# A transformer block in float32: fixed probability buffers taken in turn, with the order of two writes declared

## The chip, the core and the metric

The kernel runs on one core of a Trainium2 chip, as one launch. The core has a matrix engine (TensorE, "PE" in the profile; its weight loads are listed apart as "PEld"), a vector engine (VectorE, "DVE"), an activation engine (ScalarE, "ACT"), a general one (GpSimd, "POOL") and a sync engine ("SP"), which here issues all transfers to and from memory. Each engine works through its own list of instructions in order; one engine waits for another by semaphores. The metric is the time of one execution in device microseconds.

## The reference

One block with adaptive layer norm, for 2048 tokens of width 512: multi-head attention with 32 heads of width 16, then a two-layer network with the Mish activation and an inner width of 1792. All in float32.

```python
mod = (_silu(c) @ w_mod).reshape(c.shape[0], 6, 1, -1)
sa, ca, ga, sb, cb, gb = (mod[:, 0], mod[:, 1], mod[:, 2], mod[:, 3], mod[:, 4], mod[:, 5])
h = _layernorm(x, axis=-1) * (1 + ca) + sa
x = x + ga * _A_ref(h, A_wqkv, A_wo)      # softmax attention
h = _layernorm(x, axis=-1) * (1 + cb) + sb
x = x + gb * _B_ref(h, B_w1, B_b1, B_w2)  # Dense, Mish, Dense
```

What the change touches lies in the attention: scores = q k / 4, p = softmax(scores), o = p v.

## The kernel before, in words

**Precision.** Most operands are split into a high and a low part (names ending in `h` and `l`, or in `_h` and `_l`), and a product is made of three matmuls of such parts (`mm3`, L111). GpSimd, ScalarE and VectorE make the parts (`hi_copy` L89, `lo_sub` L97).

**Stages.** A set-up (L309 to L446) normalizes x, makes the first slices of k, q and v and stores them in DRAM scratch (`kscr`, `qscr`, `vscr`). At its end `constants()` (L405) issues transfers that fill rows of `qa` (L398), `qscr` (L409) and `vscr` (L410) with zeros, all copied from one tile `zer`. The tiles of the set-up lie in a pool `lp` that is closed at its end. Then the pools `kq2` (three more `ka` tiles) and `ap` (L451) are opened, in the space that `lp` left. The pool `ap` is opened with `reuse_waits="tile"`: an instruction that first writes a tile of it waits for what last used the memory there, whether of `ap` or of `lp`.

The main loop (L1212) goes over steps t = -20 to 513. Steps 0 to 511 are 32 iterations n of 16 steps: an iteration is four heads and 512 query tokens, a step on average one block of 128 key tokens. A step has

- four scores, so that two steps make the eight of four heads and two key blocks (`score`, L503): a matmul of k and q into one bank of `ring` and ScalarE's exponential (L510) from it into a probability buffer `pr`;
- four maxima (`max_tile`, L462) for the iteration that comes 20 steps later: a matmul (L470) into a bank of `ring` and VectorE's maximum over it (L472) into the tile `mx`, from which the rows of maxima are later made that the scores subtract;
- the values' product of step t - 2 (`pv`, L517): four matmuls (L525) that read the four `pr` buffers and the values `vg`;
- a part of other work: projections, weight preparation and the two-layer network of an earlier block of 512 tokens, cut into units (`queue`, `next_part`).

Steps -20 to -1 have maxima and whole units alone (`whole_units`), among them the values' projections (`v_unit`, L262; matmuls by L126).

**Order.** The order is written out by hand (`tc.manual_schedule()`, L49): each engine runs its instructions in the order in which the program lists them, and the hooks `at(h, ...)` set at which half step something is issued. So nothing is moved by a planner; what can differ is what an instruction waits for, and where the pool puts a tile.

**Banks.** `ring` (L144) has six banks of 128 x 512 float32, taken in turn by scores, maxima and a few others. A product that takes a bank waits until what last read it has done so.

**The probability buffers.** There are four heads in an iteration. For head 2j + s there are 3 + s buffers (14 in all), taken in turn by the pool: each call of `ap.tile(..., tag=..., bufs=3 + s)` gives the next. A new exponential into a buffer waits for the values' product that last read it and for the exponential that last wrote it. After the loop, `tail()` (L876) takes eight more tiles of the same tags for the last block's y and xn.

Of the kernel before, what the change touches and what calls it, by code (L numbers as in the profile page):

```python
# [8 lines left out]
F32 = mybir.dt.float32  # L9
# [9 lines left out]
def adaln_block(ctx: ExitStack, tc: tile.TileContext, x, wqkv, wo, w1, b1, w2, c, w_mod, out):  # L19
    nc = tc.nc  # L20
    P = 128
    S, D = x.shape[1], x.shape[2]
# [5 lines left out]
    TB = 512  # L28
# [4 lines left out]
    T = 16 * NIT  # L33
# [66 lines left out]
    def layernorm(pool, xt, xn, eng="v"):  # L100
        st = pool.tile([P, 6], F32, tag="ln_st", name="ln_st", bufs=4)
        mv = pool.tile([P, 2], F32, tag="ln_mv", name="ln_mv", bufs=4)
        rs = pool.tile([P, 2], F32, tag="ln_rs", name="ln_rs", bufs=4)
        nc.vector.bn_stats(out=st, in_=xt)
        nc.vector.bn_aggr(out=mv, in_=st)
        nc.gpsimd.tensor_scalar(rs[:, 0:1], mv[:, 1:2], 1.0, EPS, op0=ALU.mult, op1=ALU.add)
        nc.gpsimd.tensor_tensor(rs[:, 1:2], rs[:, 0:1], nhalf, op=ALU.pow)
        eng = nc.vector if eng == "v" else nc.gpsimd
        return lambda: eng.tensor_scalar(xn, xt, mv[:, 0:1], rs[:, 1:2], op0=ALU.subtract, op1=ALU.mult)
# [28 lines left out]
    def pe_run():  # L138
        while pe_queue:
            mm_go(pe_queue.pop(0))  # L140
# [6 lines left out]
    def ring(w=1):  # L147
        if w == 2 and ring_at[0] % 2:
            ring_at[0] += 1
        b = ring_at[0] % NRING  # L150
        ring_at[0] += w
        return ring_t[:, b, :] if w == 1 else ring_t[:, b:b + 2, :]

    def bank(tag="ms"):
        return ring() if tag == "ring" else ps.tile([P, TB], F32, tag=tag, name="bk", bufs=1)
# [153 lines left out]
    with ExitStack() as es:  # L309
# [28 lines left out]
        e = lp.tile([P, DK], F32, name="sil_e")  # L338
# [39 lines left out]
        pr, pm = [], ring()[:, :2 * DK].rearrange("p (i k) -> p i k", k=DK)  # L378
# [72 lines left out]
    ap = ctx.enter_context(tc.tile_pool(name="ap", bufs=1, reuse_waits="tile"))  # L451
# [46 lines left out]
                        mt[o:o + 8, :].bitcast(F32))  # L498
        at(2 * (16 * n + 16 - PRO) + 3, put)

    pts = {}

    def score(n, j, s, kc):  # L503
        def product():
            kt, qt = ka[(2 * n + j) % NR], qa[(2 * n + j) % NR]
            p_ = ring()
            nc.tensor.matmul(p_, kt[64 * s:64 * s + 64, kc * P:(kc + 1) * P], qt[64 * s:64 * s + 64, :],  # L507
                             start=True, stop=True)
            pr = ap.tile([P, TB], F32, tag=f"p{2 * j + s}", name="pr", bufs=3 + s)
            e = nc.scalar.activation(pr, p_, AF.Exp, scale=SCALE)  # L510
            pts[16 * n + kc, 2 * j + s] = pr
            return e
        return product
# [67 lines left out]
    def evac_last(ps_):  # L581

        ot, od, rb = mst["last"]
        oh, ol = o_hl[NB - 1]
        r = slice(64, P)
        dn, on = ps_
        pick = mst["pick"]
        nc.tensor.matmul(dn[r, :], pick[:, 1, :], ot, start=True, stop=True)
        nc.tensor.matmul(on[r, :], pick[:, 0, :], ot, start=True, stop=True)
        nc.vector.reciprocal(rb[r], dn[r, :])  # L590
        nc.vector.tensor_mul(od[r], on[r, :], rb[r])
        hi_copy("v", oh[r, DK - 1, :], od[r])
        lo_sub("v", ol[r, DK - 1, :], od[r], oh[r, DK - 1, :])
# [67 lines left out]
    def load_w2(f):  # L661
        return load_split("w2", NA, w2scr[f])
# [14 lines left out]
    def put_h(hh, hl, acc, k, tail):  # L677
        hf = mst["p"].tile([P, TB], F32, tag="ee", name="hf2", bufs=2)
        nc.scalar.activation(hf, acc, AF.Identity, scale=modc[:, 3, k:k + 1], bias=modc[:, 2, k:k + 1])
        hi_copy("p", hh[:, k, :], hf)  # L680
        lo_sub("v" if tail else "p", hl[:, k, :], hf, hh[:, k, :])

    def up_mms(acc, w, hh, hl):
        mm3(acc, [w1v(w, 0, k) for k in range(DK)], [w1v(w, 1, k) for k in range(DK)],
            [hh[:, k, :] for k in range(DK)], [hl[:, k, :] for k in range(DK)], "b")

    def mish(f, acc, tail):

        mp = mst["p"]
# [176 lines left out]
    def w1_tail(f):  # L866
        i, j = divmod(f % 8, 2)
        return load_w1(f) if i == 1 else half_tile(ka[(1, 0, 2, 3)[i]], j, w1scr[f])
# [7 lines left out]
    def tail():  # L876

        oh, ol = o_hl[last]
        mp = mst["p"]
        y, xn = [], []  # L880
        for v in (y, xn):
            for i in range(4):
                v.append(ap.tile([P, D], F32, tag=f"p{i}", name="y", bufs=3 + i % 2))
        for i in range(4):
            r = 4 * last + i
            nc.sync.dma_start(y[i], x[r * P:(r + 1) * P, :])
        for f in range(4, 8):
            w1s[f] = w1_tail(f)
        accs4 = [bank("ms"), bank("acc")] + [None, None]

        def wo_mms(i, ks):
            s = slice(i * P, (i + 1) * P)
            seq = [(l, r, k) for l, r in ((oh, 0), (oh, 1), (ol, 0)) for k in ks]
            for j, (l, r, k) in enumerate(seq):
                nc.tensor.matmul(accs4[i], l[:, k, s], wos[k][:, r, :], start=(k == 0 and j == 0),
                                 stop=(k == 3 and j == 2))

        wo_mms(0, (0, 1, 2))
        t = ring(2)
        evac_last([t[:, i, :] for i in range(2)])  # L900
        wo_mms(1, (0, 1, 2))
        for i in (2, 3):
            accs4[i] = bank("ring")
            wo_mms(i, (0, 1, 2))
        app = []
        for i in range(4):
            wo_mms(i, (3,))
            nc.vector.tensor_add(y[i], accs4[i], y[i])
            app.append(layernorm(mp, y[i], xn[i]))
            if i:  # L910
                app[i - 1]()
        app[3]()

        def held(js):
            t = ring(2)
            fins = []
            for i, j in enumerate(js):
                fins.append(mst["held"](j, t[:, i, :]))
                pe_run()
            return fins  # L920

        for js in ((0, 1), (2, 3)):
            for f in held(js):
                f(None)
        hh, hl = [mp.tile([P, DK, TB], F32R, tag=f"h2_{v}", name="h2", bufs=1) for v in range(2)]
        fins = held((4,))
        accs = [bank(("ring", "ms", "ring", "acc")[k]) for k in range(DK)]
        for k in range(DK):
            for i in range(4):
                nc.tensor.transpose(accs[k][:, i * P:(i + 1) * P], xn[i][:, k * P:(k + 1) * P], ident)  # L930
        for k in range(DK):
            put_h(hh, hl, accs[k], k, True)
        fins += held((5, 6))
        for f in fins:
            f(None)
        for f in held((7,)):
            f(None)
        for f in range(6):
            w2s[f] = load_w2(f)
        po = [ring(2) for _ in range(2)]  # L940
        free2 = ring(2)
        act, stages = {}, {}
        LAG = 4
        for u in range(FT + LAG):
            if u < FT:
                acc = free2[:, u // 2 % 2, :] if u % 2 else bank(("ms", "acc")[u // 2 % 2])
                up_mms(acc, w1s.pop(u), hh, hl)
                pe_run()
                if u + 8 < FT:
                    w1s[u + 8] = w1_tail(u + 8)  # L950
                act[u], stages[u] = mish(u, acc, True)
            for d, ss in ((2, (4, 5)), (1, (2, 3)), (0, (0, 1))):
                if 0 <= u - d < FT:
                    for q in ss:
                        stages[u - d][q]()
            f = u - LAG
            if f >= 0:
                a_h, a_l = act.pop(f)
                w = w2s.pop(f)
                for i in range(4):  # L960
                    s = slice(i * P, (i + 1) * P)
                    for j, (l, r) in enumerate(((a_h, 0), (a_h, 1), (a_l, 0))):
                        nc.tensor.matmul(po[i // 2][:, i % 2, :], l[:, s], w[:, r, :], start=(f == 0 and j == 0),  # L963
                                         stop=(f == FT - 1 and j == 2))
                    if f == FT - 1 and i % 2:
                        for q in (i - 1, i):
                            nc.vector.tensor_add(y[q], po[q // 2][:, q % 2, :], y[q])
                            r = 4 * last + q
                            nc.sync.dma_start(out[r * P:(r + 1) * P, :], y[q])
                if f + 6 < FT:  # L970
                    w2s[f + 6] = load_w2(f + 6)
# [276 lines left out]
```

## Time and profile before

| what | value |
|---|---|
| median of 3 runs | 1747.17 us (1742.92 to 1755.66) |
| span of the profiled execution, first to last instruction | 1752.7 us |
| its mean granted TensorE clock | 0.996 |
| instructions in it | 33365 |
| VectorE busy | 1464.5 us (84%) |
| GpSimd busy | 751.4 us (43%) |
| DMA, mean | 137 GB/s, 240.05 MB |

The profiled execution's own time is not listed apart from its span; the span lies between the lowest and the highest run.

The views that are used below: the page, with busy times and the costliest groups of instructions (line, engine, operation, tiles and shapes, count, then busy time and mean of one, then idle time in front and what ended it); the table of waits (who waited for whom, total us, times, longest); the timeline of an engine (start and length in us, then in brackets the idle time before and what ended it); the chain of work that ended last, cut to a stretch; and busy times by stretches. "SPq" and "ACTq" are the queues of the sync engine and of ScalarE: instructions that issue transfers or only wait, which are not counted as busy. "x4" after a row is the number of instructions merged in it.

### The profile page before, as it was taken

The page shows a single profiled execution, that of the slowest core. Times are in us where ns is not written, and L with a number is a line of the kernel's source. Part 1 is how long each engine was busy: PE and PEld are TensorE (multiplying, and loading weights), DVE is VectorE, ACT ScalarE, POOL GpSimd, SP SyncE. Part 2 cuts the span into 40 slices and gives each one's busy share as a digit, 9 for nine tenths or more (in the row PEclk, how much of TensorE's full clock was granted, in tenths as well). Part 3 has the DMA queues.
Part 4 walks back from the last instruction along what each step waited for, and adds up shares of the span by engine and source line. Part 5 has one row for each costly group of instructions (what it writes and reads, how often), then busy time and mean ns, then how long its engine had stood idle before and what let it go on. Part 6 is the DMA issues. An engine that isn't in the chain of part 4 may idle for free.

```text
span 1752.7 us, 33365 instructions
## 1 busy us (share of the span) xinstructions
PE 1711.7 (98%) x12230; PEld 954.7 (54%) x12230; DVE 1464.5 (84%) x2464; ACT 1341.6 (77%) x2565; POOL 751.4 (43%) x740
## 2 busy tenths in 40 slices
PE   7999999999999999999999999999999999999999
PEld 5755665555435455555455455555455455554687
DVE  6888888887888998888989898888989899891477
ACT  6247777777777898797877898797877799897464
POOL 5145224656303275263312276173412267162852
PEclk9999999999999999999999999999999999999999
DMA  7676467777662342432435443442435434422451
GB/s 236 181 234 196 119 170 208 236 238 220 207 196 63 110 117 71 143 101 67 104 108 144 126 114 80 121 120 52 120 82 158 113 102 102 126 79 71 153 228 61
DMA packets 113996, 240.05 MB, mean 137 GB/s; under 512 B 24048, under 2 KB 49648, under 8 KB 107784
## 3 DMA queue, kind: packets, MB, share of 16 engines
q1 hardware_dynamic: 113832, 237.92, 47.5%
q8 instruction: 96, 1.57, 0.4%
q14 instruction: 68, 0.56, 0.1%
HBM read 179.95 MB, written 51.44 MB: 132 GB/s over the span
## 4 chain that ended last, share of the span: by engine, by line
PE 80%; DMA 6%; DVE 4%; ACT 3%; POOL 3%; issue 2%; SPq 2%; POOLq 0%; ACTq 0%; DVEq 0%
PE bk L525 26%; PE ring L470 20%; PE ring L507 18%; PE bk L132 11%; DVE mx L472 3%; ACT pr L510 2%; DMA qscr<-ql 2%; PE ring L126 2%; PE ring L963 1%; PE bk L126 1%; DMA kscr<-ql 1%; DMA wr<-in_A_wqkv 1%; DMA w2scr<-hl 1%; DMA vg<-vscr 0%; SPq L317 0%
## 5 line engine op out<-in xcount | busy, mean ns | idle before, releaser
L472 DVE TENSOR_REDUCE mx<-ring 128x1 f32<-128x512 f32 x2048 | 1273.9, 683 | 176.9 <-PE ring L470 145.1
L510 ACT ACTIVATE pr<-ring 128x512 f32<-128x512 f32 x2048 | 1080.7, 604 | 274.7 <-PE bk L132 148.2
L470 PE MATMUL ring<-ka,qa 64*128 64x512 f32 x2048 | 847.6, 431 | 1.1 <-DVE mx L472 0.2
L507 PE MATMUL ring<-qa,ka 64*128 64x512 f32 x2048 | 737.4, 401 | 11.8 <-ACT pr L510 10.5
L470 PEld LDWEIGHTS ring<-ka,qa 64*128 64x128 f32 x2048 | 364.8, 184 | 398.3 <-DVE mx L472 321.8
L525 PE MATMUL bk<-pr,vg 128*32 128x512 f32 x4096 | 547.0, 606 | 0.0
L507 PEld LDWEIGHTS ring<-qa,ka 64*128 64x128 f32 x2048 | 372.5, 185 | 119.9 <-ACT pr L510 64.3
L132 PE MATMUL bk<-h,w 64*128 64x512 f32 x996 | 275.9, 409 | 1.4 <-ACT pr L510 1.2
L132 PEld LDWEIGHTS bk<-h,w 64*128 64x128 f32 x996 | 171.1, 184 | 17.5 <-ACT pr L510 7.7
L132 PE MATMUL bk<-w,a_h 64*128 64x512 f32 x576 | 167.2, 414 | 0.3
L525 PEld LDWEIGHTS bk<-pr,vg 128*32 128x32 f32 x4096 | 80.7, 108 | 138.6 <-issue 133.4
L830 POOL TENSOR_TENSOR y<-yd,y 128x512 f32<-128x512 f32 x40 | 51.9, 1303 | 214.2 <-ACT yd L829 193.6
L711 POOL TENSOR_TENSOR hb<-hb,ee 128x512 f32<-128x512 f32 x42 | 53.9, 1284 | 178.2 <-DVE ee L710 178.2
L132 PEld LDWEIGHTS bk<-w,a_h 64*128 64x128 f32 x576 | 96.4, 184 | 12.0 <-ACT pr L510 6.7
L724 POOL TENSOR_TENSOR qq<-ee,rr 128x512 f32<-128x512 f32 x42 | 54.4, 1295 | 75.3 <-ACT rr L717 72.7
L132 PE MATMUL bk<-w,o_hl 64*128 64x512 f32 x288 | 80.6, 411 | 1.6 <-POOL o_hl L95 1.0
L132 PE MATMUL bk<-w,a_l 64*128 64x512 f32 x288 | 76.9, 390 | 0.0
L98 POOL TENSOR_TENSOR a_l<-hb,a_h 128x512 fp32r<-128x512 f32 x53 | 72.3, 1363 | 4.4
L132 PE MATMUL bk<-h_h,wl 64*128 64x512 f32 x168 | 57.2, 421 | 0.0
L710 DVE SCALAR_TENSOR_TENSOR ee<-ee 128x512 f32<-128x512 f32 x56 | 39.8, 711 | 19.3 <-ACT ee L707 19.3
L727 POOL TENSOR_TENSOR hb<-hb,rr 128x512 f32<-128x512 f32 x42 | 54.4, 1296 | 3.3
L132 PEld LDWEIGHTS bk<-w,a_l 64*128 64x128 f32 x288 | 53.0, 184 | 4.8
(186 smaller groups left out, 1735.8 us busy)
## 6 DMA issues: line engine op xcount, KB each, us to landing
ka<-kscr SPq DMA_DIRECT2D x124, 384.0 KB
w<-w2scr SPq DMA_DIRECT2D x56, 512.0 KB
w<-w1scr SPq DMA_DIRECT2D x46, 512.0 KB
vg<-vscr SPq DMA_DIRECT2D x32, 552.0 KB
qa<-qscr SPq DMA_DIRECT2D x124, 100.0 KB
kscr<-qh SPq DMA_DIRECT2D x16, 512.0 KB
qscr<-qh SPq DMA_DIRECT2D x32, 256.0 KB
hl<-in_B_w SPq DMA_DIRECT2D x28, 256.0 KB
```

Source lines behind the costliest of these rows:

```text
L98: (nc.gpsimd if eng == "p" else nc.vector).tensor_sub(lo, src, hi.bitcast(F32))
L126: nc.tensor.matmul(acc, l, r, start=start, stop=stop)
L132: i = nc.tensor.matmul(acc, l[64 * g:64 * g + 64], r[64 * g:64 * g + 64], start=start, stop=stop)
L470: nc.tensor.matmul(pm, qt[64 * s:64 * s + 64, qs * P:(qs + 1) * P], kt[64 * s:64 * s + 64, kb * TB:(kb + 1) * TB], start=True, stop=True)
L472: nc.vector.tensor_reduce(out=mxs[n][:, s, 4 * j + qs, kb:kb + 1], in_=pm, op=ALU.max, axis=AX.X)
L507: nc.tensor.matmul(p_, kt[64 * s:64 * s + 64, kc * P:(kc + 1) * P], qt[64 * s:64 * s + 64, :], start=True, stop=True)
L510: e = nc.scalar.activation(pr, p_, AF.Exp, scale=SCALE)
L525: nc.tensor.matmul(accs[n][32 * h:32 * h + 32, :], vgs[n][:, o:o + 32], pts.pop((t, h)), start=(kc == 0), stop=(kc == 15))
L711: (nc.vector if tail else nc.gpsimd).tensor_mul(hb, hb, ee)
L724: nc.gpsimd.tensor_mul(qq, ee, rr)
L727: nc.gpsimd.tensor_mul(hb, hb, rr)
L830: nc.gpsimd.tensor_add(y[i], yd, y[i])
```

## The change

The 14 probability buffers are made once, as tiles of `ap` with names of their own, in front of the loop, and the step picks one by (16 n + kc) mod (3 + s). For each buffer the last exponential is remembered (`exps`), and the next one into the same buffer is declared to have no dependency on it, since the values' product between them, which reads the first and is waited for by the second, orders them. The tail picks its y and xn from the same list. The buffers have the same sizes and number as before; they are now made ahead of every other tile of `ap`.

```diff
-    pts = {}
+    pts, exps = {}, {}
+    prs = [[ap.tile([P, TB], F32, name=f"pr{i}_{b}") for b in range(3 + i % 2)] for i in range(4)]
 
     def score(n, j, s, kc):
         def product():
...
             p_ = ring()
             nc.tensor.matmul(p_, kt[64 * s:64 * s + 64, kc * P:(kc + 1) * P], qt[64 * s:64 * s + 64, :],
                              start=True, stop=True)
-            pr = ap.tile([P, TB], F32, tag=f"p{2 * j + s}", name="pr", bufs=3 + s)
+            pr = prs[2 * j + s][(16 * n + kc) % (3 + s)]
             e = nc.scalar.activation(pr, p_, AF.Exp, scale=SCALE)
+            k = 2 * j + s, (16 * n + kc) % (3 + s)
+            if k in exps:
+                tc.declare_no_dep(e.ins, exps[k].ins, reason="the values' product between them reads it")
+            exps[k] = e
             pts[16 * n + kc, 2 * j + s] = pr
             return e
         return product
...
         oh, ol = o_hl[last]
         mp = mst["p"]
-        y, xn = [], []
-        for v in (y, xn):
-            for i in range(4):
-                v.append(ap.tile([P, D], F32, tag=f"p{i}", name="y", bufs=3 + i % 2))
+        y, xn = ([prs[i][(T + v) % (3 + i % 2)] for i in range(4)] for v in range(2))
```

## The prediction

> **What bounds the kernel now.** I read the page first: busy time and the costliest groups.
>
> ```profile
> span 1752.7 us, 33365 instructions
> PE 1711.7 (98%) x12230; PEld 954.7 (54%) x12230; DVE 1464.5 (84%) x2464; ACT 1341.6 (77%) x2565; POOL 751.4 (43%) x740
> L472 DVE TENSOR_REDUCE mx<-ring 128x1 f32<-128x512 f32 x2048 | 1273.9, 683 | 176.9 <-PE ring L470 145.1
> L510 ACT ACTIVATE pr<-ring 128x512 f32<-128x512 f32 x2048 | 1080.7, 604 | 274.7 <-PE bk L132 148.2
> ```
>
> TensorE has almost no idle time. The change touches ScalarE's 2048 exponentials (L510), and ScalarE sits idle for 274.7 us in front of them, mostly until TensorE hands it a bank. So ScalarE has slack, and an edit to it counts only where TensorE waits for an exponential. The table of waits shows how often that is (line waited for: us in total, times, longest).
>
> ```profile
> PEld ring L470 <- DVE mx L472: 321.8, 402, 0.8
> PEld ring L507 <- ACT pr L510: 64.3, 96, 2.6
> PEld ring L470 <- ACT pr L510: 26.3, 59, 0.8
> PEld bk L132 <- ACT pr L510: 14.5, 15, 1.5
> PE ring L507 <- ACT pr L510: 10.5, 36, 2.1
> ```
>
> Those are 96 + 59 + 15 + 36 = 206 waits for an exponential, against 402 for a maximum on VectorE, the engine with the next-highest load.
>
> **What the change takes away.** In the listing of the built kernel before, 549 of the 2048 exponentials wait for ScalarE itself: for the earlier exponential into the same buffer, at least 10 ScalarE instructions back. Such a wait is over before it is asked for, but 547 of these exponentials now carry two waits, and then the one for TensorE stands in an instruction of its own in front. After the change none of them does; every instruction of the five engines otherwise stands in the same order. I looked at one exponential with the extra instruction and at one without, each after an idle stretch of ScalarE: the product that it reads, the wait instruction, the exponential (timeline and the line's own view).
>
> ```profile
> L510 ACTq EVENT_SEMAPHORE  x553: 17/17/1687, 111.4 to 1616.7; - x185
> 704.53 0.39 PE L507 MATMUL ring<-qa,ka 64*128 64x512 f32 x1
> L510 ACTq EVENT_SEMAPHORE  x1: 17/17/17, 705.0 to 705.0; - x1
> 705.02 0.60 ACT L510 ACTIVATE pr<-ring 128x512 f32<-128x512 f32 x1 [1.03 <-PE bk L132]
> 707.58 0.39 PE L507 MATMUL ring<-qa,ka 64*128 64x512 f32 x1
> 708.00 0.60 ACT L510 ACTIVATE pr<-ring 128x512 f32<-128x512 f32 x1 [0.43 <-PE bk L132]
> ```
>
> With it, the exponential starts 705.02 - (704.53 + 0.39) = 0.10 us after its product ends; without it, 708.00 - (707.58 + 0.39) = 0.03 us. So the wait instruction costs 0.07 us, and only where ScalarE was idle and waiting for TensorE; behind a running exponential it is hidden. If every one of the 553 lay on the path that would be 38.7 us; that is the upper bound of the gain, and zero the lower. A share of 553/2048 of TensorE's 206 waits gives 206 x 0.27 x 0.07 = 3.9 us. I take 2 us, because behind a freed wait the next thing late is usually a maximum (402 waits).
>
> The Trainium skill, page "VectorE: DVE Perf Modes", section "The DRAIN you can't avoid", speaks against even this: there a chain of copies takes the same time with a semaphore after each as with one at the end, "the semaphore costs nothing extra here". It was measured on VectorE; carried over to ScalarE it makes this term 0 and the sum 2 us worse. The rows above disagree for an engine that was idle.
>
> The other edits I cost at nothing. Thirty-one ScalarE instructions elsewhere (L271, L539, L793, L91) gain a wait for an exponential 37 or more places back, long done; 0.017 us each in front of idle time. The last token block's y and xn take the same buffers in turn as before. That all tiles of the pool move to other addresses has no row of its own; I leave it at zero, and the range covers it.
>
> **What the change adds.** The 14 buffers are now the pool's first tiles, at its low end, and push the maxima's tile mx to a higher address. Before, mx lay over an input tile that had long been read; now it lies over zer, the tile of zeros that the set-up's fills are copied from. In the listing of the changed kernel the first maximum (L472) therefore waits for eight DMAs: the last of L398 (rows of qa), four of L409 (qscr), and L410 (vscr); before it waited for its product alone. (Three of these waits stood on the fifth exponential, at 111 us, when they were long over.) Here is that place: first VectorE, then TensorE, then the DMA issues of the sync engine, then the landing of the last fill in the chain of waits.
>
> ```profile
> 53.84 12.24 DVE L472 TENSOR_REDUCE mx<-ring 128x1 f32<-128x512 f32 x20
> 66.25 2.48 DVE L472 TENSOR_REDUCE mx<-ring 128x1 f32<-128x512 f32 x4 [0.17 <-PE ring L470]
> 55.11 0.73 PE L470 MATMUL ring<-ka,qa 64*128 64x512 f32 x4
> 57.75 0.73 PE L470 MATMUL ring<-ka,qa 64*128 64x512 f32 x4
> 65.05 3.73 SPq L398 DMA_DIRECT2D qa<-zer x6
> 68.83 3.53 SPq L409 DMA_DIRECT2D qscr<-zer x4
> 72.40 0.59 SPq L410 DMA_DIRECT2D vscr<-zer x1
> 72.40 2.54 DMA vscr<-zer
> 75.13 3.82 SPq L1205 DMA_DIRECT2D ka<-ka x6
> ```
>
> The last fill lands at 72.40 + 2.54 = 74.94 us, and nothing ahead of it in the sync engine's queue waits for VectorE's maxima, so it lands then in the changed kernel too. The first maximum moves from 53.84 to about 75.05, 21.2 us later. Behind it on VectorE stand all the other maxima; TensorE waits for them by the ring's six banks. Four are filled by the first group of products and two by the next (the group at 55.11); the third and fourth of that group then need the banks of the first two maxima. The maxima follow each other at 12.24/20 = 0.61 us, so the second ends near 75.05 + 0.61 + 0.68 = 76.34, and the fourth product starts near 76.4 where it started at 55.11 + 0.73 - 0.39 = 55.45. TensorE is 20.9 us late. The values' projections stand behind these products in TensorE's queue, their copies on ScalarE behind them, and the vscr writes (L278) behind those. No spare time takes this back at once: each step here lasts 57.75 - 55.11 = 2.64 us, TensorE has no gap in it, and VectorE waits 0.17 us per step for TensorE.
>
> A stall also costs clock. After gaps of 2.88 and 2.48 us TensorE ran at half speed (columns: the stretch and its length, busy time of PE, PEld, DVE, ACT and POOL, then granted clock, DMA share, GB/s).
>
> ```profile
> 97.45 0.96 PE L126 MATMUL bk<-h_h,wh 128*128 128x512 f32 x3 [2.88 <-ACT ql L242]
> 410.03 0.79 PE L132 MATMUL bk<-h_h,wh 64*128 64x512 f32 x1 [2.48 <-ACT ql L242]
> 75.00:103.00 28.00, 25.12 (x117) 16.33 (x115) 22.43 (x39) 4.13 (x8) 10.07 (x10) 0.94 1.00 262
> 97.00:103.00 6.00, 5.55 (x20) 3.50 (x20) 3.00 (x6) 1.50 (x3) 5.00 (x5) 0.72 0.91 277
> 405.00:418.00 13.00, 10.52 (x62) 5.25 (x58) 6.94 (x12) 6.58 (x13) 6.04 (x7) 0.74 0.67 232
> 83.40 0.62 ACT L91 CAST wh<-wr 128x512 fp32r<-128x512 f32 x1 [4.60 <-DMA wr<-in_A_wqkv]
> 84.09 1.28 POOL L98 TENSOR_TENSOR wl<-wr,wh 128x512 fp32r<-128x512 f32 x1 [29.01 <-ACT wh L91]
> 87.38 9.33 DMA kscr<-ql
> 59.65 3.30 DMA kscr<-ql
> ```
>
> Lost were (1 - 0.72) x 6 = 1.7 us and (1 - 0.74) x 13 = 3.4 us. For the new stall I take the middle, 2.6.
>
> Part comes back later. The 2.88 us gap before 97.45 and its 1.7 us of clock come from one store of kscr that took 9.33 us, while the same store took 3.30 us at 59.65. It stood in a jam: from 75 to 103 us the DMA engines are fully busy, first with the ka copies (L1205, issued from 75.13) and the next weight slice, whose late arrival also held ScalarE 4.60 us and put GpSimd's split of it (1.28 us) ahead of the store's data. In the changed kernel those copies and that load run while TensorE stalls, some 20 us earlier beside the work that follows, so I take the store to be done in time: 2.9 + 1.7 = 4.6 us back.
>
> The sum: 20.9 + 2.6 - 4.6 - 2.0 = +16.9 us on the profiled span of 1752.7. That span lies inside the three runs (1742.92 to 1755.66), and what lies around it isn't shown; I add the sum to the median: 1747.2 + 16.9 = 1764.1. One per cent, about what a measurement of this kernel can tell from no change, is 17.5 us.
>
> **The rivals.** First: the stall is not made up for. The jam stays, because the sync engine's next loads keep their order and the share is 1.00 for 28 us. Then the sum is 20.9 + 2.6 - 2.0 = +21.5, 1768.7. Against it: the copies from 75.13 on are out of it.
>
> Second, the other side: not slower, but faster. The wait instructions on ScalarE sit in the round trip from product to exponential to freed bank, and all 553 count: -38.7 + 18.9 = -19.8, 1727.4. It decides from 18.9/0.07 = 270 of them on the path; the page has TensorE waiting for exponentials only 206 times, in all cases together.
>
> Third: the change doesn't do what the listing says, and the first maximum's wait is short, because fills and maxima do not meet on the chip as they do in the trace of before. What is left is the gain: -2, 1745.2. Against it: L410's issue at 72.40 is on the sync engine's own path.
>
> Fourth, the zero gain: every removed wait was covered by another, a maximum's or ScalarE's own queue; +18.9, 1766.1. The rule quoted above from the Trainium skill's page "VectorE: DVE Perf Modes" comes to the same.
>
> **How the numbers follow.** My forecast has 0.60. Its ends are 20.9 + 1.7 - 4.6 - 3.9 = +14.1 and 20.9 + 3.4 - 4.6 = +19.7, across the one-per-cent bound: 0.35 within, 0.25 over. The first rival has 0.20, 0.18 of it over; the second 0.05; the third 0.07, within; the fourth 0.08, over. So faster 0.05, within 1% 0.35 + 0.02 + 0.07 = 0.44, slower 0.25 + 0.18 + 0.08 = 0.51. The range goes from +14.1 less the 4.3 us by which the lowest run lies under the median, and a little for the addresses (1754), to the worst sum, 20.9 + 3.4 = +24.3 with nothing back, and 3 us for the runs (1775).
>
> **What would show it.** In the changed kernel's profile: the first L472 starts near 75, with DMA vscr<-zer as what it waited for, and TensorE has a gap of some 19 us from about 56; granted clock near one half follows. The gap of 2.88 us in front of L126 is gone. The L126 group that follows it, now at 97.45, starts near 97.45 - 2.9 + 20.9 + 2.6 = 118. Wait instructions in front of exponentials fall from 553 to a handful, and late exponentials start 0.03 us after their product. A first maximum near 54, or waits for exponentials in the hundreds that vanish, would make me wrong.

## The result, and the profile after

| | median | runs |
|---|---|---|
| before | 1748.16 us | 6 (1742.92 to 1755.66) |
| changed | 1761.99 us | 6 (1760.90 to 1767.22) |
| ratio | 1.0079 | 95% interval 1.0059 to 1.0099 |

The changed kernel is 13.8 us slower. That is clear of the scatter of its runs, and under the one per cent that the prediction set as its bound.

The page of the changed kernel, the lines that answer to those shown before:

```profile
span 1759.8 us, 32836 instructions
PE 1702.9 (97%) x12230; PEld 945.4 (54%) x12230; DVE 1463.3 (83%) x2464; ACT 1340.4 (76%) x2565; POOL 751.4 (43%) x740
L472 DVE TENSOR_REDUCE mx<-ring 128x1 f32<-128x512 f32 x2048 | 1273.0, 681 | 187.3 <-PE ring L470 141.8
L511 ACT ACTIVATE pr<-ring 128x512 f32<-128x512 f32 x2048 | 1080.0, 604 | 268.3 <-PE bk L132 144.8
```

The work is the same; the trace holds 33365 - 32836 = 529 instructions fewer, and TensorE's busy time has fallen from 1711.7 to 1702.9 us while the span has grown. That looks like something gained all along the kernel and something larger lost in one place. The table of waits names the place:

```profile
PEld ring L470 <- DVE mx L472: 342.3, 410, 17.4
PEld ring L508 <- ACT pr L511: 64.9, 96, 3.5
DVE mx L472 <- DMA vscr<-zer: 18.0, 1, 18.0
```

There is one wait of VectorE for the fill of `vscr`, 18.0 us long, which the kernel before did not have; and the longest of the waits of TensorE's weight loads for a maximum is now 17.4 us, where it was 0.8. The timeline there, VectorE, TensorE and the sync engine's issues:

```profile
69.48 4.87 DVE L472 TENSOR_REDUCE mx<-ring 128x1 f32<-128x512 f32 x8 [18.00 <-DMA vscr<-zer]
52.68 0.49 PE L470 MATMUL ring<-ka,qa 64*128 64x512 f32 x2
70.22 1.39 PE L470 MATMUL ring<-ka,qa 64*128 64x512 f32 x2 [17.05 <-DVE mx L472]
75.04 0.87 PE L470 MATMUL ring<-ka,qa 64*128 64x512 f32 x4
60.45 3.73 SPq L398 DMA_DIRECT2D qa<-zer  x6
64.23 2.51 SPq L409 DMA_DIRECT2D qscr<-zer  x4
66.78 0.59 SPq L410 DMA_DIRECT2D vscr<-zer  x1
```

TensorE fills two more banks at 52.68 and then stands for 17.05 us, until the first maxima give banks back. Of the eight maxima that follow each other in 4.87 us, six had their banks filled by then. The fills are issued in the same order as before; only now the first maximum waits for them. The waits in front of the exponentials, in the view of their line:

```profile
L511 ACTq EVENT_SEMAPHORE  x4: 17/17/17, 212.6 to 1593.4; - x4
```

553 have become 4.

### The profile page after: what moved, and what is told of

Same layout as the page of the kernel before. It is cut to its first block, busy times and chain, and to the rows that moved or that the text cites. A ratio compares the mean times of both kernels' runs of the same rounds, so it can differ in the third digit from the quotient of the medians.

```text
span 1759.8 us, 32836 instructions
## 1 busy us (share of the span) xinstructions
PE 1702.9 (97%) x12230; PEld 945.4 (54%) x12230; DVE 1463.3 (83%) x2464; ACT 1340.4 (76%) x2565; POOL 751.4 (43%) x740
## 4 chain that ended last, share of the span: by engine, by line
PE 81%; DMA 6%; ACT 4%; POOL 3%; DVE 3%; SPq 1%; issue 1%; POOLq 0%; ACTq 0%; DVEq 0%
PE bk L530 26%; PE ring L470 20%; PE ring L508 18%; PE bk L132 10%; PE bk L126 3%; ACT pr L511 2%; PE ring L126 2%; DVE mx L472 1%; PE ring L965 1%; DMA w2scr<-hl 1%; DMA xt<-in_A_x 1%; DMA hl<-in_B_w 1%; DMA kscr<-qh 1%; DMA qscr<-ql 1%; DMA wm<-in_w_mod 1%
## 5 line engine op out<-in xcount | busy, mean ns | idle before, releaser
L470 PE MATMUL ring<-ka,qa 64*128 64x512 f32 x2048 | 842.5, 428 | 18.2 <-DVE mx L472 17.2
L470 PEld LDWEIGHTS ring<-ka,qa 64*128 64x128 f32 x2048 | 365.3, 184 | 414.3 <-DVE mx L472 342.3
L508 PEld LDWEIGHTS ring<-qa,ka 64*128 64x128 f32 x2048 | 372.4, 185 | 122.7 <-ACT pr L511 64.9
L835 POOL TENSOR_TENSOR y<-yd,y 128x512 f32<-128x512 f32 x40 | 51.9, 1304 | 212.7 <-ACT yd L834 192.2
L731 POOL TENSOR_TENSOR rr<-rr,qq 128x512 f32<-128x512 f32 x42 | 54.0, 1286 | 3.5
```

The costliest lines, as they stand in the source:

```text
L470: nc.tensor.matmul(pm, qt[64 * s:64 * s + 64, qs * P:(qs + 1) * P], kt[64 * s:64 * s + 64, kb * TB:(kb + 1) * TB], start=True, stop=True)
L731: nc.gpsimd.tensor_mul(rr, rr, qq)
```

## The experiments

Three theories were on the table. The first is the prediction's: a loss from the first maximum's wait for the fills, a gain from the wait instructions that left ScalarE. The second: those instructions were worth nothing, and the loss alone is seen. The third: the loss comes from where the buffers lie.

### Buffers made at their first use

The change as it is, but each buffer is made when it is first written, so that `mx` is made ahead of them and lies where it lay before.

```diff
-    prs = [[ap.tile([P, TB], F32, name=f"pr{i}_{b}") for b in range(3 + i % 2)] for i in range(4)]
+    prs = {}
...
-            pr = prs[2 * j + s][(16 * n + kc) % (3 + s)]
+            k = 2 * j + s, (16 * n + kc) % (3 + s)
+            if k not in prs:
+                prs[k] = ap.tile([P, TB], F32, name=f"pr{k[0]}_{k[1]}")
+            pr = prs[k]
...
```

> Fixed buffers and the declared order as in the change, but each buffer is made at its first use, so that the tile of the maxima keeps its old, low address. First theory (the loss is the first maximum's wait for the fills, the gain is the wait instructions in front of the exponentials): first maximum near 54 us with no DMA wait in front, no gap of 17 us on TensorE, waits of the exponentials as in the changed kernel; 1742 to 1746 us against 1748 before. Second theory (the removed wait instructions are worth nothing, as a rule of the Trainium skill has it): 1748 us, same as before.

Measured: 1742.41 us against 1747.86 before, ratio 0.9972 (0.9960 to 0.9984). The first maximum is back, by the timeline, with nothing waited for, and of the wait instructions in front of exponentials 6 are left (the line's row stands further down):

```profile
52.02 12.25 DVE L472 TENSOR_REDUCE mx<-ring 128x1 f32<-128x512 f32 x20
70.67 0.59 SPq L410 DMA_DIRECT2D vscr<-zer  x1
95.66 0.96 PE L126 MATMUL bk<-h_h,wh 128*128 128x512 f32 x3 [2.90 <-DMA kscr<-qh]
```

So the change has a gain of its own, 5.4 us by the medians, and its loss is not in the buffers or in the declaration but in the order in which tiles are made. This version is faster than both kernels, than the one before by 0.3%. (The third row is the gap that the prediction meant to see go; more on it below.)

### Buffers made first, the waits left in

The changed kernel without the declaration.

```diff
-            if k in exps:
-                tc.declare_no_dep(e.ins, exps[k].ins, reason="the values' product between them reads it")
```

> The changed kernel without the declaration: buffers made first, the 549 waits of exponentials for ScalarE back in place. First theory: the loss without the gain, 1764 to 1768 us. Second theory: as the changed kernel, 1762 us.

Measured: 1768.23 us, ratio 1.0112 (1.0095 to 1.0129), 0.2 us above the range that was expected; its line has 551 wait instructions. That is 6.2 us above the changed kernel: the same gain, seen from the other side, as far as intervals of some 3 us for each kernel can tell. The loss stands there too:

```profile
L511 ACTq EVENT_SEMAPHORE  x551: 17/17/1708, 134.3 to 1629.4; - x184
71.61 4.87 DVE L472 TENSOR_REDUCE mx<-ring 128x1 f32<-128x512 f32 x8 [17.85 <-DMA vscr<-zer]
72.36 1.39 PE L470 MATMUL ring<-ka,qa 64*128 64x512 f32 x2 [15.57 <-DVE mx L472]
```

### Only the maxima made low

The changed kernel with two fixed tiles for the maxima made in front of the buffers; all the rest stays where the change put it, to within 512 bytes.

```diff
+    mxb = [ap.tile([P, 2, 8, 4], F32, name=f"mx{b}") for b in range(2)]
     prs = [[ap.tile([P, TB], F32, name=f"pr{i}_{b}") for b in range(3 + i % 2)] for i in range(4)]
...
-            mxs[n] = ap.tile([P, 2, 8, 4], F32, tag="mx", name="mx", bufs=2)
+            mxs[n] = mxb[n % 2]
```

> The changed kernel with only the two tiles of the maxima made ahead of the probability buffers; every other tile of the pool keeps the changed kernel's place to within 512 bytes. First theory: as the kernel with buffers made at their first use, 1742 to 1746 us. Third theory (the loss comes from where the probability buffers or the values lie, not from the wait): 1760 to 1764 us.

Measured: 1745.20 us, ratio 0.9984 (0.9971 to 0.9997), with the first maxima at 51.9 us:

```profile
51.90 12.24 DVE L472 TENSOR_REDUCE mx<-ring 128x1 f32<-128x512 f32 x20
```

Moving tiles of 512 bytes per partition takes the whole loss away. The buffers, `vg` and the small tiles lie as in the changed kernel, so the third theory falls. Whether the 2.8 us to the first experiment mean anything can't be said; the two intervals overlap.

### A wait on nearly every exponential

The first experiment's kernel, with each exponential made to wait for the one two before it on ScalarE, which has ended.

```diff
...
+            back.append(e)
+            if len(back) > 2:
+                tc.add_manual_dep(e.ins, back[-3].ins.name,
+                                  mybir.DependencyInfo(mybir.DependencyClass.Sync, mybir.DependencyReason.DATA),
+                                  reason="the exponential before the last one")
```

> The kernel with buffers made at their first use, and nearly every exponential made to wait for the one two before it, which has ended: 1986 wait instructions more on ScalarE than without. First theory: TensorE waits for an exponential some 206 times, 0.07 us later each time, so 14 us or a little more above that kernel, 1756 to 1762 us. Second theory: nothing, 1742 to 1748 us.

Measured: 1761.12 us, ratio 1.0075 (1.0061 to 1.0088), 18.7 us above the first experiment. Its line and that of the first:

```profile
L514 ACTq EVENT_SEMAPHORE  x2012: 17/17/1667, 106.7 to 1642.6; - x183
```

```profile
L514 ACTq EVENT_SEMAPHORE  x6: 17/17/38, 111.6 to 1574.2; - x6
```

18.7 us for 2006 wait instructions are 9 ns each; 5.4 us for the 553 - 6 of the kernel before are 10 ns each. By the intervals of the ratios the first figure is uncertain by 1 to 2 ns and the second by about 4, so the price is the same at a quarter of the dose and at the full one as far as this can tell. The second theory falls: a wait that is over when it is asked for is not free here. The 18.7 us are also more than the 14 us that TensorE's listed waits for exponentials allow. Where the rest is, the page's groups tell. First the kernel before, then the first experiment, then this one:

```profile
L470 PE MATMUL ring<-ka,qa 64*128 64x512 f32 x2048 | 847.6, 431 | 1.1 <-DVE mx L472 0.2
```

```profile
L470 PE MATMUL ring<-ka,qa 64*128 64x512 f32 x2048 | 840.9, 428 | 1.1 <-DVE mx L472 0.2
```

```profile
L470 PE MATMUL ring<-ka,qa 64*128 64x512 f32 x2048 | 857.4, 436 | 0.9 <-DVE mx L472 0.2
```

The idle time in front of the maxima's products has not grown; they have become "longer": 840.9 us of busy time with 6 wait instructions, 847.6 with 553, 857.4 with 2012. The last two experiments, further down, fit in: first the one with 4 wait instructions, then the one with 553.

```profile
L469 PE MATMUL ring<-ka,qa 64*128 64x512 f32 x2048 | 840.7, 428 | 1.1 <-DVE mx L471 0.2
```

```profile
L470 PE MATMUL ring<-ka,qa 64*128 64x512 f32 x2048 | 847.0, 431 | 1.1 <-DVE mx L472 0.2
```

The timelines at the end of a step show how, first without the waits, then with them:

```profile
1468.25 0.43 PE L470 MATMUL ring<-ka,qa 64*128 64x512 f32 x1
1468.26 0.39 PE L508 MATMUL ring<-qa,ka 64*128 64x512 f32 x1
1468.61 1.07 PE L532 MATMUL bk<-pr,vg 128*32 128x512 f32 x8
```

```profile
1486.66 0.39 PE L508 MATMUL ring<-qa,ka 64*128 64x512 f32 x1
1486.68 0.47 PE L470 MATMUL ring<-ka,qa 64*128 64x512 f32 x1
1487.08 1.07 PE L537 MATMUL bk<-pr,vg 128*32 128x512 f32 x8
```

A score and a maximum's product run side by side, each on 64 rows of the array (they start 0.01 to 0.02 us apart). With the waits, the maximum's product (L470) is listed as longer, 0.47 us instead of 0.43, and the values' product follows 0.42 us after the pair's first start instead of 0.36. No idle time of TensorE is listed there, since one of the pair is always running. Only this place was looked at so closely; that the whole difference comes about in this way is inferred from the busy times.

### The fills behind the copies

The first experiment's kernel with the set-up's fills moved, in the sync engine's queue, behind the ka copies and the weight slice's load. The zeros come from the second gate's tile, which is free until then.

```diff
-        zer = lp.tile([P, TB], F32, name="zer")
+        zer = gates[1]
...
-        constants()
         slice_split(1, 1)
...
     at(-2 * PRO, lambda: slice_load(*plan[2][1:3]))
+    at(-2 * PRO, constants)
```

> The kernel with buffers made at their first use, and the set-up's fills moved behind the ka copies and the weight slice's load in the sync engine's queue (copied from the second gate's tile, which is empty till then, in place of zer). If the gap of 2.9 us on TensorE near 96 us and the half clock after it come from these copies and this load standing in the jam of the DMA engines, as the prediction's term of 4.6 us back has it: no gap over 1 us between 60 and 110 us, and 1738 to 1741 us where that kernel had 1742.4. If the jam is made by the loads and stores behind them: the gap stays, and so does the time.

Measured: 1742.15 us against 1749.21 before on that chip, ratio 0.9965 (0.9953 to 0.9976). In the profiled execution there is no gap over 1 us in that stretch; but the time lies above the expected 1741, and by the ratios it cannot be told from the first experiment. The next experiment shows why this one is inconclusive.

### Fixed buffers at their first use, with the waits

The first experiment's kernel without the declaration (the same two lines out).

> Fixed buffers made at their first use, without the declaration: the 549 waits are back, the maxima lie low. First theory: neither loss nor gain, 1746 to 1750 us, as before. If fixed buffers or their new places are worth something by themselves, it shows here.

Measured: 1748.97 us against 1749.21, ratio 0.9998 (0.9987 to 1.0009). Fixed buffers and their places are worth nothing that these runs can tell. The waits are back, by the line's row:

```profile
L514 ACTq EVENT_SEMAPHORE  x553: 17/17/1708, 108.3 to 1607.4; - x185
```

Its profile has no gap over 1 us near 96 us, though its set-up is that of the kernel before. The first maximum and the last fill's landing, from its timeline and its chain:

```profile
51.61 2.47 DVE L472 TENSOR_REDUCE mx<-ring 128x1 f32<-128x512 f32 x4
```

```profile
66.73 2.51 DMA vscr<-zer
```

The last fill lands 66.73 + 2.51 - 51.61 = 17.6 us after the first maximum. In the profiled execution of the kernel before it was 74.94 - 53.84 = 21.1, and in that of the first experiment 70.67 + 2.50 - 52.02 = 21.2 (its chain has the 2.50). These last two have the gap of 2.9 us; with 17.6 it is absent. The experiments "Only the maxima made low" and "A wait on nearly every exponential" have no gap over 1 us there either. Their last fill is issued like this, the second with its first maximum in front:

```profile
66.91 0.59 SPq L410 DMA_DIRECT2D vscr<-zer  x1
```

```profile
53.30 12.25 DVE L472 TENSOR_REDUCE mx<-ring 128x1 f32<-128x512 f32 x20
68.06 0.59 SPq L410 DMA_DIRECT2D vscr<-zer  x1
```

Counted to this issue, the last fill came 66.91 - 51.90 = 15.0 and 68.06 - 53.30 = 14.8 us after the first maximum, and 66.73 - 51.61 = 15.1 in this experiment; in the kernel before and in the first experiment it was 72.40 - 53.84 = 18.6 and 70.67 - 52.02 = 18.7. So the gap goes with executions in which the set-up's transfers run late, whatever the kernel. That is five executions, two with the gap and three without; why the transfers run late in some is open.

## Why the prediction was right

The forecast was 1764 us, the measurement 1762. The place of the loss, its cause and the direction of both large terms stood. That the sum came so close is in part luck: two terms, each off by some 4 us, cancel, and the gain was put at less than half of what it is. Of its two likeliest outcomes the prediction gave the larger chance, 0.51, to a loss of over one per cent; what came is the other, within one per cent, with 0.44. Its terms, one by one:

**The first maximum's wait (predicted +20.9).** Right in place, cause and what stands behind it: VectorE from the fill's landing on, TensorE after two more banks. The size was 17.05 us in the changed kernel and 15.57 with the waits left in. The term was worked out from one execution with a late set-up, 21.1 us; in the changed kernel's the last fill landed at 66.78 + 2.52 = 69.30, some 17.8 us after the maximum could have started (69.48 - 18.00 = 51.48). The prediction's own sign, a group of L126 products near 118 us, was missed by 6: the group started at 111.83 (its row stands below), since the wait was 3.9 us shorter and the set-up reached the first maximum 53.84 - 51.48 = 2.4 us earlier.

**The clock (predicted +2.6).** Half clock lasted after the restart at 70.22, by the windows view (same columns as in the prediction):

```profile
70.00:76.00 6.00, 5.78 (x22) 4.43 (x23) 4.64 (x9) 0.37 (x1) 0.00 (x0) 0.55 0.88 145
```

(1 - 0.55) x 6 = 2.7 us, close to the 2.6 forecast.

**What comes back (predicted -4.6).** The changed kernel's profile has indeed no gap there. In the kernel before, one of ScalarE's copies waited for a store; in the changed kernel they wait for TensorE. First the kernel before, then the changed one:

```profile
96.81 0.59 ACT L242 COPY ql<-bk 128x512 f32<-128x512 f32 x1 [9.74 <-DMA kscr<-ql]
```

```profile
100.28 0.59 ACT L242 COPY ql<-bk 128x512 f32<-128x512 f32 x1 [3.53 <-PE bk L126]
103.91 0.59 ACT L242 COPY ql<-bk 128x512 f32<-128x512 f32 x1 [3.04 <-PE bk L126]
108.44 0.59 ACT L242 COPY ql<-bk 128x512 f32<-128x512 f32 x1 [3.95 <-PE bk L126]
```

But three of the five profiles named above have no such gap either, without any stall, so in the medians little of it can come back. Between kernels that differ in the tiles' order alone, the loss is 1762.0 - 1742.4 = 19.6 us without the waits (16.8 against the third experiment's 1745.2) and 1768.2 - 1749.0 = 19.2 with them. That fits the stall and its clock, 17.05 + 2.7 = 19.8, with nothing to subtract; but by the intervals each of these differences is uncertain by about 4 us, and 19.8 - 4.6 = 15.2 is not excluded by them alone.

The traces say more. This is the group of L126 products that stood behind the gap in the kernel before, at 97.45: in the changed kernel, in the one with the waits left in, and in the third experiment.

```profile
111.83 0.85 PE L126 MATMUL bk<-h_h,wh 128*128 128x512 f32 x3
```

```profile
113.94 0.85 PE L126 MATMUL bk<-h_h,wh 128*128 128x512 f32 x3
```

```profile
93.27 0.96 PE L126 MATMUL bk<-h_h,wh 128*128 128x512 f32 x3 [0.64 <-ACT ql L242]
```

From the moment at which the first maximum could start, the group comes after 111.83 - 51.48 = 60.35 us in the changed kernel, after 113.94 - 53.76 = 60.18 with the waits left in (53.76 is 71.61 less the 17.85 of idle), and after 93.27 - 51.90 = 41.37 in the third experiment, which has no such gap. In the kernel before, which has it, it is 97.45 - 53.84 = 43.61. So the stall costs the same in both kernels that have it, although the idle time listed for it differs by 1.5 us: some 19 us against an execution without the gap, and 16.7 against one with it (the clock that the gap costs is lost only behind this group). The prediction's "comes back" holds against the one execution that it was read from, and not against the kernel. How many of the executions behind the medians have the gap isn't shown.

The late set-up that made the first term too large by 3.9 also went with the gap that this one counted on. The two errors cancel, and that is luck: 20.9 - 4.6 = 16.3 beside 17.05.

**The wait instructions (predicted -2.0).** The right mechanism, mis-sized: 5.4 to 6.2 us, above even the upper share of 3.9. The step that failed is counting TensorE's listed waits for an exponential, 206 of them. Those hardly changed (96 waits of 64.3 us at the scores' weight loads before, 96 of 64.9 after); the gain came out of pairs of matmuls whose waits are not listed. The quoted rule of the Trainium skill's page "VectorE: DVE Perf Modes", section "The DRAIN you can't avoid", that a semaphore costs nothing extra, is measured there for one at each operation's end on VectorE. For a wait in front of ScalarE's exponentials the runs decide otherwise, with some 10 ns each.

**The addresses (predicted 0).** Nothing that could be told, by fixed buffers at places of their own (ratio 0.9998, 0.9987 to 1.0009).

**The rivals.** The first, that nothing comes back, has the better account, by the profiles without the gap, but its total of 21.5 was too high through the first term and the gain. The second is out: 547 waits are worth 5 us, not 38.7. The third is out by the changed kernel's own waits. The fourth, no gain, is out by three experiments. The sum remade with the measured terms is 17.05 + 2.7 - 5.8 = +14.0 (5.8 is the middle of 5.4 and 6.2), and 13.8 was measured; that they are so close means little, with an interval of 10.3 to 17.3 us around the 13.8.

## What to carry to other kernels

In a pool like this one, whose tiles wait for what last used their memory, the order in which tiles are made sets which old tile's readers a new tile waits for; a fixed tile that is made early for tidiness can push a small, urgent one onto memory that slow transfers still read. After such an edit, look in the built program for waits that the first writers have gained, and make a tile near its first use, or the most urgent first. And a sum of terms from a single profiled execution can be right while its terms are not: take a second execution before you count on a gap of a few microseconds to close.

## What the runs showed of the hardware

- A wait that has ended, if it makes a wait instruction of its own in front of an activation, cost 9 to 11 ns on average over the kernel, in two doses (547 and 2006). In the one pair of exponentials that was compared in the kernel before, both after idle time of ScalarE, it was 0.07 us.
- Short waits of TensorE between matmuls that run side by side on 64 rows each did not show as idle time here; they showed as longer busy time of one of the two lines (840.7 to 840.9 us with 4 and 6 wait instructions on ScalarE, 847.0 to 847.6 with 553, 857.4 with 2012). At one place this was seen directly; for the rest it is inferred.
- Half clock followed gaps of 2.88 and 2.48 us in the kernel before: the granted clock was 0.72 over the 6 us around the end of the first and 0.74 over 13 us around the second. The Trainium skill, page "TensorE: Matmul & The Clock Gate", section "Part 1: The HAM clock gate (the "warmup" mystery)", has the clock fall after at least one idle window of about 3.4 us; here shorter gaps were enough, and the measurement decides.
